# Reordering the 2,285 tasks of a delta-rule and gated feed-forward kernel, and which of its two DMA queues issues what

## The chip, the core and the metric

The kernel runs on one core of one Trainium2 chip. A core has TensorE (PE in the profile; PEld is its loading of weights), VectorE (DVE), ScalarE (ACT), GpSimd (POOL) and SyncE (SP), each with its own instruction stream that is worked off in order, and 16 DMA engines that all queues share. The metric is device time of one launch in microseconds (us). The kernel before took 643.51 us (median of three runs: 641.13, 643.51, 645.41).

## The reference, cut to what matters

```python
# q, k, v: (4, 8, 768, 48); beta: (4, 8, 768)
k_n = k / (norm(k) + 1e-06)
for t in range(768):                     # a state of 48 x 48 per batch and head
    y[t] = q[t] @ state
    v_old = state.T @ k_n[t]
    state = state + beta[t] * outer(k_n[t], v[t] - v_old)
x = y as (3072 tokens, 384)
h = x @ w_in                             # 384 x 2048
out = (h * cos(h)) @ w_out               # 2048 x 384
```

(The layer works on all 2048 columns; the weights arrive as 64-bit numbers, of which the kernel makes 32-bit ones.)

## The kernel before, in words

**The work.** The recurrence is done in 24 chunks of 32 time steps, for all 32 pairs of batch and head at once. For chunk n, in short:

- `k`, `q`, `v` n: DMAs that load the chunk (`load`, L393; 4 DMAs each, 8 for `k` from chunk 6 on).
- `turn` n (L677) turns k and q on TensorE for the first six chunks, and `turn_out` copies them out of PSUM on ScalarE. From chunk 6 on there is no turn on TensorE: `blocks` n 0 and 1 (L421, 4 DMAs each) load k and q in pieces of 32 wide, and `turn_out` n is `turn_blocks` (L697): four transposes of VectorE that write the tile `kq_t`.
- `gram` n (L704) multiplies keys with keys and queries; `gram_keys` and `gram_queries` (L839) take it out of PSUM on VectorE.
- The inverse of a triangular matrix: chunks 0 and 1 by repeated doubling on TensorE (`double`, L788, six levels of two halves, with copies, transposes and sums between). For chunk pairs m from 1 on: `gram_put` writes the matrices to DRAM, `gram_get` m reads them in another layout, POOL inverts (`inv`, L898), `put` m writes the result to DRAM, `get` n (L924) reads it back into the tile `zt`, of which there is one.
- `state` n (L946), `right` n, `solve` n (L1015) on TensorE; `solve_out` on VectorE (L1053); `part_out` on ScalarE (L1062, its copies L1066); `update` n (L1068) on TensorE and `update_out` on VectorE, which writes the state that `state` n+1 reads. Chunks 2 and 3 have `solve_half` and `between` ahead of `solve`.
- `within` n (L1087), `within_out` on ScalarE, `features` n (L1121) turn the chunk's answer into columns of x, `features_out` copies them.

Two chunks make a pair p of 256 tokens for the feed-forward part. Pair 0 goes through `hidden` (L1143: a quarter of a hidden block of 512 columns each) and `output` (L1343, an output column's 16 matmuls one by one, f = 0 to 15, for two halves of the tokens). The other pairs use sums of inputs and of weights (`x_sum` L1229, `in_sums` L1276, `left_sum` L1412, `right_sum`), so that fewer products are needed: 20 `layer` tasks per pair (L1318, four matmuls each) with `layer_copy` on ScalarE (L1334) and `layer_add` on VectorE, and seven `product` tasks of two parts each (L1399, four matmuls per part), which `collect` (L1436; ScalarE L1442, VectorE L1455) adds up in one of two output tiles `o`. `store` p i (L1464) writes a tile to DRAM, which frees it. The gate h cos(h) between is `turns` (L1185), `rest` (L1192), `cos` (L1201) and `gate` (L1204).

The weights come in 28 pieces (`weights` t, `narrow_load`, L547): t = 0 to 11 belong to the first matrix, t = 12 to 27 to the second one, and piece 12 + f is read by output column f. Each piece is a DMA and three steps that make 32-bit numbers of it: `split` on ScalarE, `shift` on VectorE, `add` on POOL.

**What sets the order.** Every step is registered as a task with `add`: a key such as `("get", 11)`, the engine, what it depends on, and which buffers it makes and uses. 2,285 tasks are registered. `Order.run` (L227) then emits them one after the other in the order that is written out in `LINE`, a list of the tasks' numbers:

```python
line = [keys[int(i)] for i in self.LINE.split()]
for key in line:
    emit, deps, makes, uses = self.tasks[key]
    assert deps <= done, key
    ...
    emit()
```

So `LINE` fixes the order on every engine, and which buffer a task gets (the one freed longest ago). The set `OTHER` holds the keys of the tasks that go to the second of two places: for a transfer, ScalarE's queue in place of SyncE's (`queue`, L387); for a sum, POOL in place of VectorE or the reverse (`either`, L390); for `within_half`, ScalarE in place of VectorE.

```python
def queue(*key):
    return nc.scalar if key in Order.OTHER else nc.sync
```

At the end every instruction is pinned behind the one before it on its engine (`pin`, L1971), and the DMAs of SyncE and ScalarE are pinned in the one order in which `LINE` has them, also across the two queues. In the trace these DMAs signal their end on eight semaphores in turn, so a DMA that is issued waits until the eighth one before it has landed. There are 666 of them, 101 issued by ScalarE.

**Warm-ups.** `keep_warm` (L501) is a matmul of no use on a tile of ones, which does nothing once the first output column has begun. Five stand ahead of all tasks (`WARM_FIRST`); 15 more are tasks `warm` 0 to 14 (`WARMS`). Nine of these 15 stand ahead of the first output column in `LINE`.

Of the kernel before, what the change touches and what calls it, by code (L numbers as in the profile page):

```python
# [60 lines left out]
class Order:  # L61

    OTHER = {
        ('double_eye', 0), ('double_far', 0), ('double_eye', 1), ('gram_put', 3), ('inv', 1, 0),
        ('inv', 1, 2), ('put', 1), ('within_half', 3), ('gram_put', 4), ('k', 5),
        ('gram_get', 2), ('put', 2), ('v', 9), ('put', 4), ('gram_put', 10), ('blocks', 11, 1),
        ('put', 5), ('get', 14), ('v', 15), ('gram_put', 15), ('blocks', 16, 1), ('get', 18),
        ('k', 19), ('v', 19), ('get', 20), ('put', 10), ('get', 21), ('get', 22), ('v', 23),
        ('blocks', 23, 0), ('put', 11), ('store', 0, 0), ('in_sums', 0), ('in_sums', 1),
        ('x_sum', 1, 'd'), ('x_sum', 1, 'n'), ('x_sum', 1, 'm'), ('x_sum', 1, 'e'),  # L70
        ('x_sum', 1, 'k'), ('x_sum', 1, 'g'), ('x_sum', 1, 'i'), ('x_sum', 1, 'l'),
        ('x_sum', 1, 'f'), ('x_sum', 1, 'h'), ('x_sum', 1, 'b0'), ('left', 1, 2, 0),
        ('left', 1, 3, 0), ('left', 1, 3, 1), ('x_sum', 2, 'd'), ('x_sum', 2, 'n'),
        ('x_sum', 2, 'm'), ('x_sum', 2, 'e'), ('x_sum', 2, 'k'), ('x_sum', 2, 'g'),
        ('x_sum', 2, 'l'), ('left', 2, 4, 0), ('left', 2, 4, 1), ('x_sum', 3, 'd'),
        ('x_sum', 3, 'n'), ('x_sum', 3, 'm'), ('x_sum', 3, 'e'), ('x_sum', 3, 'k'),
        ('x_sum', 3, 'g'), ('x_sum', 3, 'i'), ('x_sum', 3, 'l'), ('x_sum', 3, 'h'),
        ('left', 3, 1, 1), ('left', 3, 3, 0), ('x_sum', 4, 'd'), ('x_sum', 4, 'n'),
        ('x_sum', 4, 'm'), ('x_sum', 4, 'k'), ('x_sum', 4, 'g'), ('x_sum', 4, 'i'),
        ('x_sum', 4, 'f'), ('x_sum', 4, 'h'), ('x_sum', 4, 'b0'), ('left', 4, 3, 0),  # L80
        ('left', 4, 3, 1), ('store', 4, 0), ('x_sum', 5, 'd'), ('x_sum', 5, 'n'),
        ('x_sum', 5, 'm'), ('x_sum', 5, 'g'), ('x_sum', 5, 'i'), ('x_sum', 5, 'l'),
        ('left', 5, 1, 0), ('left', 5, 3, 0), ('left', 5, 3, 1), ('store', 5, 0),
        ('x_sum', 6, 'd'), ('x_sum', 6, 'n'), ('x_sum', 6, 'e'), ('x_sum', 6, 'k'),
        ('x_sum', 6, 'g'), ('x_sum', 6, 'i'), ('left', 6, 4, 1), ('left', 6, 3, 1),
        ('store', 6, 1), ('x_sum', 7, 'd'), ('x_sum', 7, 'm'), ('x_sum', 7, 'k'),
        ('x_sum', 7, 'g'), ('x_sum', 7, 'l'), ('x_sum', 7, 'b0'), ('left', 7, 2, 0),
        ('left', 7, 3, 0), ('x_sum', 8, 'e'), ('x_sum', 8, 'k'), ('x_sum', 8, 'g'),
        ('x_sum', 8, 'i'), ('left', 8, 2, 0), ('left', 8, 2, 1), ('left', 8, 4, 1),
        ('left', 8, 3, 1), ('store', 8, 0), ('x_sum', 9, 'n'), ('x_sum', 9, 'k'),  # L90
        ('x_sum', 9, 'g'), ('x_sum', 9, 'i'), ('x_sum', 9, 'l'), ('x_sum', 9, 'f'),
        ('x_sum', 9, 'h'), ('x_sum', 9, 'b0'), ('left', 9, 1, 1), ('left', 9, 2, 1),
        ('left', 9, 3, 0), ('left', 9, 3, 1), ('store', 9, 0), ('x_sum', 10, 'n'),
        ('x_sum', 10, 'm'), ('x_sum', 10, 'k'), ('x_sum', 10, 'g'), ('x_sum', 10, 'i'),
        ('x_sum', 10, 'f'), ('left', 10, 4, 0), ('left', 10, 4, 1), ('left', 10, 3, 0),
        ('x_sum', 11, 'd'), ('x_sum', 11, 'm'), ('x_sum', 11, 'k'), ('x_sum', 11, 'i'),
        ('left', 11, 1, 0), ('left', 11, 1, 1), ('left', 11, 2, 1), ('left', 11, 4, 0),
        ('left', 11, 4, 1), ('left', 11, 3, 0), ('store', 11, 1), ('store_right', 11),
        ('weights', 2), ('weights', 4), ('weights', 5), ('weights', 9), ('weights', 11),
        ('weights', 12), ('weights', 13), ('weights', 14), ('weights', 17), ('weights', 18),  # L100
        ('weights', 20)
    }
# [1932 lines left out]
```

## Time and profile before

| | |
|---|---|
| median of three runs | 643.51 us (641.13, 643.51, 645.41) |
| the profiled execution | 639.35 us |
| its span, first to last instruction | 637.5 us |
| instructions | 24,379 |
| DMA traffic | 50.51 MB, mean 79 GB/s |

The profile is of one execution, which was faster than the median. Its lines carry an engine, the line of the code (of a helper, where one emits), the tile written and the tiles read (out<-in), the count (x4) and microseconds. PE is TensorE, PEld its weight load; SPq and ACTq are the DMA issues of SyncE and ScalarE. In a timeline the first number is the start in us from the beginning of the span and the second the duration; a bracket gives how long the engine stood idle before and what released it. In the list of waits the numbers are the total of the wait in us, how often, and the longest one. A row of a stretch A:B gives its length, then the busy time of PE, PEld, DVE, ACT and POOL with the count of instructions, the granted clock of TensorE as a share of full speed, the mean busy share of the 16 DMA engines, and GB/s.

### The profile page before, as it was taken

How to read it: one execution, taken by the hardware profiler on the slowest of the kernel's cores; microseconds unless marked ns; L12 is line 12 of the kernel's file. 1: busy time of each engine (PE TensorE's matmuls, PEld its weight loads, DVE VectorE, ACT ScalarE, POOL GpSimd, SP SyncE). 2: the span in 40 equal slices, each digit the busy share in tenths (PEclk: the TensorE clock that was granted, in tenths of full speed). 3: DMA queues.
4: the chain of work that ended last, by engine and by line, in shares of the span. 5: the costliest groups of instructions: out<-in, count | busy, mean ns of one | idle time of the engine just before them, and what ended most of it. 6: DMA issues, size and time to landing. Idle time of an engine off the chain costs nothing.

```text
span 637.5 us, 24379 instructions
## 1 busy us (share of the span) xinstructions
PE 604.4 (95%) x10276; PEld 561.9 (88%) x10276; DVE 484.1 (76%) x981; ACT 326.1 (51%) x608; POOL 436.1 (68%) x774
## 2 busy tenths in 40 slices
PE   7788897999999998899999999999999999999997
PEld 6567776886999998889999999999999999999997
DVE  6878865989999886677978788867778576645772
ACT  3746664554753653553853645655453454545440
POOL 5468888688888886884987887878866862121222
PEclk9999998999999999999999999999999999999999
DMA  8878665665645444327436254323232101100001
GB/s 178 209 182 208 142 130 128 142 86 75 105 83 89 70 68 97 68 35 127 64 53 112 46 90 83 62 35 68 47 56 54 34 6 21 35 3 25 1 26 26
DMA packets 215893, 50.51 MB, mean 79 GB/s; under 512 B 207512, under 2 KB 210856, under 8 KB 215784
## 3 DMA queue, kind: packets, MB, share of 16 engines
q1 hardware_dynamic: 175600, 37.10, 31.8%
q10 hardware_dynamic: 39976, 11.61, 8.7%
q8 instruction: 81, 1.33, 0.9%
q0 software_dynamic: 208, 0.25, 0.2%
q14 instruction: 28, 0.23, 0.1%
HBM read 38.68 MB, written 10.22 MB: 77 GB/s over the span
## 4 chain that ended last, share of the span: by engine, by line
PE 69%; DMA 13%; DVE 6%; SPq 5%; issue 2%; ACT 2%; POOL 1%; ACTq 1%; DVEq 0%; POOLq 0%
PE p_h L1322 26%; PE p_out L1403 24%; PE p_kq L959 3%; DMA qp<-in_k_dram 3%; PE p_s L1075 2%; DMA out_dram<-o 2%; DMA kp<-in_k_dram 2%; PE p_out L1345 2%; DMA qp<-in_q_dram 2%; SPq L427 2%; PE p_kq L1092 2%; PE p_g L715 2%; PE p_h L1403 2%; PE p_u L1033 2%; SPq L408 1%
## 5 line engine op out<-in xcount | busy, mean ns | idle before, releaser
L908 POOL TENSOR_TENSOR part<-z,gb 128x126 f32<-128x126 f32 (+24 forms) x317 | 141.0, 445 | 36.9 <-DMA gb<-g_dr 6.6
L915 POOL TENSOR_TENSOR z<-z,part 128x126 f32<-128x126 f32 (+24 forms) x317 | 145.4, 459 | 24.8
L1403 PE MATMUL p_out<-w_out,g_ffn 128*128 128x192 f32 x672 | 120.3, 328 | 0.1
L1403 PEld LDWEIGHTS p_out<-w_out,g_ffn 128*128 128x128 f32 x672 | 107.9, 190 | 1.0 <-ACT o L1442 0.2
L1322 PE MATMUL p_h<-x_sum,w_in 128*128 128x128 f32 x704 | 93.9, 279 | 0.9 <-DVE g_ffn L1339 0.5
L1185 ACT ACTIVATE turns<-g_ffn,quarter_turn 128x512 int32<-128x512 f32 x77 | 55.4, 721 | 76.5 <-DVE g_ffn L1339 27.4
L1201 ACT ACTIVATE turns<-turns,halfpi 128x512 f32<-128x512 f32 x96 | 68.4, 719 | 50.6 <-DVE turns L1192 43.4
L1322 PEld LDWEIGHTS p_h<-x_sum,w_in 128*128 128x128 f32 x704 | 86.2, 191 | 4.6 <-DVE g_ffn L1339 0.8
L1403 PE MATMUL p_out<-w_sum,g_ffn 128*128 128x192 f32 x496 | 88.2, 328 | 1.8 <-DVE o L1455 1.7
L1403 PEld LDWEIGHTS p_out<-w_sum,g_ffn 128*128 128x128 f32 x496 | 79.7, 190 | 2.7 <-DVE o L1455 1.9
L1339 DVE TENSOR_TENSOR g_ffn<-g_ffn,p_h 128x512 f32<-128x512 f32 x88 | 59.6, 681 | 24.5 <-PE p_h L1322 19.6
L1192 DVE SCALAR_TENSOR_TENSOR turns<-g_ffn,turns 128x512 f32<-128x512 f32 x77 | 57.2, 748 | 13.7 <-ACT turns L1185 13.1
L1204 DVE TENSOR_TENSOR g_ffn<-turns,g_ffn 128x512 f32<-128x512 f32 x77 | 58.7, 769 | 8.2 <-ACT turns L1201 8.2
L1322 PE MATMUL p_h<-x_sum,in_sum 128*128 128x128 f32 x440 | 59.1, 278 | 1.5 <-ACT p_h L1334 1.5
L1322 PEld LDWEIGHTS p_h<-x_sum,in_sum 128*128 128x128 f32 x440 | 54.6, 192 | 3.9 <-ACT p_h L1334 2.0
L1419 POOL TENSOR_TENSOR g_ffn<-g_ffn,g_ffn 128x512 f32<-128x512 f32 x20 | 26.8, 1346 | 41.1 <-PE p_out L1403 41.0
L1105 ACT COPY y<-p_kq 32x384 f32<-32x384 f32 x88 | 41.3, 470 | 19.8 <-PE p_kq L1092 17.6
L1455 DVE SCALAR_TENSOR_TENSOR o<-p_out,o 128x192 f32<-128x192 f32 x74 | 25.1, 351 | 32.1 <-PE p_out L1403 25.6
L606 POOL TENSOR_TENSOR knrm<-ksum,halves 128x16 f32<-128x16 f32 (+1 forms) x14 | 37.0, 2643 | 17.1 <-DVE ksum L594 16.4
L1322 PE MATMUL p_h<-x_ffn,w_in 128*128 128x128 f32 x352 | 46.8, 277 | 0.2 <-ACT p_h L1334 0.2
L1322 PEld LDWEIGHTS p_h<-x_ffn,w_in 128*128 128x128 f32 x352 | 43.4, 192 | 1.5 <-ACT p_h L1334 0.5
L1334 ACT COPY p_h<-p_h 128x512 f32<-128x512 f32 x44 | 25.3, 574 | 32.9 <-PE p_h L1322 22.4
(175 smaller groups left out, 1039.7 us busy)
## 6 DMA issues: line engine op xcount, KB each, us to landing
gb<-g_dr SPq DMA_DIRECT2D x18, 256.0 KB
vp<-in_v_dram SPq DMA_DIRECT2D x80, 48.0 KB
w_sum<-in_moe_w_out_dram SPq DMA_DIRECT2D x9, 384.0 KB
kp<-in_k_dram SPq DMA_DIRECT2D x136, 24.0 KB
out_dram<-o SPq DMA_DIRECT2D x16, 192.0 KB
qp<-in_k_dram SPq DMA_DIRECT2D x34, 64.0 KB
g_ffn<-in_moe_w_in_dram SPq DMA_DIRECT2D x4, 512.0 KB
qp<-in_q_dram SPq DMA_DIRECT2D x32, 64.0 KB
```

The lines of the kernel that those rows point to most:

```text
L606: nc.gpsimd.tensor_tensor(out=scales[m][2][:, part], in0=sums[m, part.start][:, 0:n], in1=halves[:, 0:n], op=ALU.pow,)
L908: eng.tensor_tensor(out=part, in0=z[:, 0:rows, j, None].to_broadcast(shape), in1=a[:, j, None, j + 1 :].to_broadcast(shape), op=ALU.mult,)
L915: eng.tensor_tensor(out=behind, in0=behind, in1=part, op=ALU.subtract)
L1105: nc.scalar.copy(by_parity(y[quarter(b)]), p_kq[quarter(b ^ 1), :, b % 2])
L1185: nc.scalar.activation(turns[p, f], hidden_of(p, f), AF.Identity, bias=quarter_turn, scale=TURN)
L1192: nc.vector.scalar_tensor_tensor(out=r, in0=hidden_of(p, f), scalar=TURN, in1=t, op0=ALU.mult, op1=ALU.subtract,)
L1201: nc.scalar.activation(r, r, AF.Sin, bias=halfpi, scale=2.0 * math.pi)
L1204: nc.vector.tensor_tensor(out=place(p, f), in0=step_of(rests.pop((p, f)), f), in1=step_of(hidden_of(p, f), f), op=ALU.mult,)
L1322: nc.tensor.matmul(p_h[:, e], in_block(*w)[:, e], x_of(p, b), start=new and e == 0, stop=True, skip_group_check=True,)
L1339: nc.vector.tensor_tensor(out=part_of(p, to), in0=part_of(p, one), in1=part_of(p, two), op=op)
L1403: nc.tensor.matmul(p_o, left(p, part, a)[:, e % 4], right(e, b), start=(e == 0), stop=(e == FT // 2 - 1), skip_group_check=True,)
L1419: either(("left", p, x, s), nc.vector, nc.gpsimd).tensor_tensor(out=left(p, s, to), in0=left(p, s, one), in1=left(p, s, two), op=op)
```

## The change: two lists and a count

The diff touches only the class `Order`. No function changes; the same tasks are emitted with the same operands.

```diff
     OTHER = {
-        ('double_eye', 0), ('double_far', 0), ('double_eye', 1), ('gram_put', 3), ('inv', 1, 0),
-        ('inv', 1, 2), ('put', 1), ('within_half', 3), ('gram_put', 4), ('k', 5),
...
-        ('weights', 2), ('weights', 4), ('weights', 5), ('weights', 9), ('weights', 11),
-        ('weights', 12), ('weights', 13), ('weights', 14), ('weights', 17), ('weights', 18),
-        ('weights', 20)
+        ('double_eye', 0), ('v', 2), ('gram_put', 2), ('within_half', 2), ('inv', 1, 0),
+        ('put', 1), ('within_half', 3), ('q', 4), ('gram_put', 4), ('gram_get', 2),
...
+        ('weights', 7), ('weights', 12), ('weights', 13), ('weights', 14), ('weights', 15),
+        ('weights', 19)
     }
 
-    WARM_FIRST, WARMS = 5, 15
+    WARM_FIRST, WARMS = 5, 20
     LINE = """
-0 26 27 9 10 11 2173 1 2 5 3 28 12 13 4 30 142 84 85 86 31 2177 143 32 2181 2185 29 89 33 35 87 174
...
```

Decoded, it comes to this.

- **Warm-ups:** 20 tasks in place of 15; 19 of them stand ahead of the first output column, where it was 9. With the five ahead of all tasks that is 24 effective ones in place of 14.
- **Queues:** ScalarE issues 128 of the 666 DMAs in place of 101: output stores 11 in place of 7, `v` 8 in place of 4, `weights` 7 in place of 11, and others. Counted in groups (one task's DMAs), ScalarE has 50 in place of 44, and from `store 0,0` on 33 in place of 25, without the last stores.
- **Sums:** of 121 `x_sum` 52 are on POOL in place of 45; of 88 `left` sums 30 in place of 33; one `right` sum, where there was none; one of `in_sums` in place of two; one of `double_eye` and `double_far` in place of three. Of the pieces of the half-size inverse (`inv 1`) one is on VectorE in place of two, of `within_half` two on ScalarE in place of one.
- **Order.** The order of all tasks. Three stretches of the DMAs follow (a star marks ScalarE's queue, the number in brackets counts the DMAs up to the task's last one):

```
up to 28, before: weights 0 (1), k 2 (5), weights 1 (6), q 2 (10), *weights 2 (11), weights 3 (12),
  k 3 (16), *weights 4 (17), q 3 (21), eye_load (22), v 0 (26), *weights 5 (27), weights 6 (28)
up to 29, after:  weights 0 (1), k 2 (5), weights 1 (6), weights 2 (7), k 3 (11), weights 3 (12),
  q 2 (16), weights 4 (17), v 0 (21), *weights 5 (22), q 3 (26), weights 6 (27), eye_load (28),
  *weights 7 (29)

101 to 152, before: *weights 18 (101), get 3 (109), weights 19 (110), *weights 20 (111),
  blocks 6,1 (115), weights 21 (116), blocks 6,0 (120), k 8 (128), weights 22 (129), blocks 7,1 (133),
  v 4 (137), blocks 7,0 (141), k 9 (149), weights 23 to 25 (152)
101 to 152, after:  *weights 18 (101), get 3 (109), blocks 6,0 (113), *weights 19 (114),
  weights 20 (115), weights 21 (116), k 8 (124), blocks 6,1 (128), blocks 7,0 (132), blocks 7,1 (136),
  *k 9 (144), v 4 (148), weights 22 (149), weights 23 to 25 (152)

320 to 418, before: get 9 (320), blocks 13,0 (324), blocks 14,0 (328), v 12 (332), gram_put 12 (335),
  k 15 (343), blocks 14,1 (347), blocks 15,0 (351), gram_put 13 (354), *put 5 (355), store 1,0 (356),
  gram_get 6 (358), get 10 (362), v 13 (366), k 16 (374), blocks 15,1 (378), get 11 (382), k 17 (390),
  store 2,0 (391), v 14 (395), k 18 (403), *k 19 (411), store 2,1 (412), gram_put 14 (415),
  *gram_put 15 (418)
320 to 417, after:  *get 9 (320), v 11 (324), blocks 14,0 (328), v 12 (332), *gram_put 12 (335),
  k 15 (343), store 1,0 (344), *v 13 (348), gram_put 13 (351), put 5 (352), gram_get 6 (354),
  blocks 14,1 (358), get 10 (362), blocks 15,0 (366), get 11 (370), k 16 (378), store 2,0 (379),
  *v 14 (383), k 17 (391), store 2,1 (392), blocks 15,1 (396), k 18 (404), gram_put 14 (407),
  *blocks 16,0 (411), gram_put 15 (414), put 6 (415), gram_get 7 (417)
```

TensorE's tasks at the start (d 0.1.0 is `double` of chunk 0, level 1, half 0; h 0.2 is part 2 of block 0 of `hidden`):

```
before: warm 0-4, turn 0, gram 0, turn 1, d 0.0.1, gram 1, d 0.0.0, d 0.1.1, warm 5, d 1.0.0, d 0.2.1,
  d 1.0.1, d 0.3.1, turn 2, d 0.1.0, d 1.1.0, gram 2, warm 6, d 0.4.1, d 0.2.0, turn 3, d 1.1.1,
  d 0.5.1, gram 3, d 0.3.0, d 1.2.0, d 1.2.1, d 0.4.0, d 0.5.0, state 0, warm 7-8, d 1.3.0, solve 0,
  update 0, d 1.3.1, within 0, d 1.4.0, turn 4, d 1.4.1, features 0, d 1.5.1, d 1.5.0, state 1,
  gram 4, h 0.0-3, solve 1
after:  warm 0-1, turn 0, warm 2, gram 0, warm 3, turn 1, gram 1, warm 4-5, d 0.0.0, d 0.0.1, warm 6-8,
  d 0.1.0, d 0.1.1, d 1.0.1, warm 9, turn 2, d 0.2.0, d 0.2.1, d 1.1.1, gram 2, d 1.0.0, turn 3,
  d 0.3.0, d 1.1.0, d 1.2.1, d 0.3.1, gram 3, d 1.2.0, d 1.3.1, d 0.4.0, warm 10, d 0.4.1, warm 11,
  state 0, d 0.5.1, d 0.5.0, d 1.4.1, warm 12, solve 0, warm 13, d 1.3.0, update 0, within 0, turn 4,
  warm 14-15, features 0, state 1, d 1.5.1, h 0.0, gram 4, d 1.4.0, h 0.1, d 1.5.0, h 0.2, solve 1
```

And what TensorE has between steps that wait for one another:

| from, to | before | after |
|---|---|---|
| solve_half 2 to between 2 | nothing | h 6.3 |
| between 2 to solve 2 | output 0,0 column 1, h 8.0, h 8.1 | h 8.0 to h 8.2 |
| solve 2 to within 2 | nothing | output 0,0 column 0, h 8.3 |
| within 2 to update 2 | nothing | h 10.0 |
| solve 4 to update 4 | output 0,0 column 12, one layer, output column 13, within 4 | one layer, within 4 |
| solve 8 to update 8 | both parts of a product of pair 2, within 8 | one layer, within 8 |
| within 8 to features 8 | update 8, six layers, both parts of a product, state 9, gram 12, solve 9 | update 8 and one layer |

Output column 10 of the first half, which reads `weights 22`, stands behind `update 3` in the new order.

More of the change, by code (lines that the diff above doesn't have):

```diff
@@ L70 @@
[L70 to L98, printed above, removed]
-        ('weights', 2), ('weights', 4), ('weights', 5), ('weights', 9), ('weights', 11),
@@ new lines @@
+        ('blocks', 20, 1), ('gram_put', 20), ('v', 21), ('gram_get', 10), ('put', 10),
+        ('v', 22), ('v', 23), ('put', 11), ('get', 23), ('store', 0, 0), ('right', 2, 2),
+        ('in_sums', 4), ('x_sum', 1, 'd'), ('x_sum', 1, 'n'), ('x_sum', 1, 'm'),
+        ('x_sum', 1, 'e'), ('x_sum', 1, 'k'), ('x_sum', 1, 'g'), ('x_sum', 1, 'i'),
+        ('x_sum', 1, 'f'), ('x_sum', 1, 'b0'), ('left', 1, 1, 0), ('x_sum', 2, 'd'),
+        ('x_sum', 2, 'n'), ('x_sum', 2, 'm'), ('x_sum', 2, 'e'), ('x_sum', 2, 'k'),
@@ new lines @@
+        ('x_sum', 2, 'g'), ('x_sum', 2, 'i'), ('x_sum', 2, 'l'), ('x_sum', 2, 'b0'),
+        ('left', 2, 4, 0), ('x_sum', 3, 'd'), ('x_sum', 3, 'l'), ('x_sum', 3, 'f'),
+        ('x_sum', 3, 'h'), ('x_sum', 3, 'b0'), ('left', 3, 4, 1), ('store', 3, 0),
+        ('store', 3, 1), ('x_sum', 4, 'i'), ('x_sum', 4, 'f'), ('x_sum', 4, 'h'),
+        ('left', 4, 4, 0), ('left', 4, 4, 1), ('left', 4, 3, 0), ('left', 4, 3, 1),
+        ('x_sum', 5, 'd'), ('x_sum', 5, 'm'), ('x_sum', 5, 'e'), ('x_sum', 5, 'k'),
@@ new lines @@
+        ('x_sum', 5, 'g'), ('x_sum', 5, 'f'), ('x_sum', 5, 'b0'), ('left', 5, 1, 0),
+        ('left', 5, 2, 0), ('left', 5, 1, 1), ('left', 5, 2, 1), ('left', 5, 4, 0),
+        ('left', 5, 3, 0), ('store', 5, 0), ('x_sum', 6, 'd'), ('x_sum', 6, 'n'),
+        ('x_sum', 6, 'm'), ('x_sum', 6, 'k'), ('x_sum', 6, 'i'), ('x_sum', 6, 'f'),
+        ('x_sum', 6, 'h'), ('x_sum', 6, 'b0'), ('left', 6, 1, 1), ('left', 6, 2, 1),
+        ('store', 6, 0), ('store', 6, 1), ('x_sum', 7, 'n'), ('x_sum', 7, 'e'),
@@ new lines @@
+        ('x_sum', 7, 'i'), ('x_sum', 7, 'h'), ('x_sum', 7, 'b0'), ('left', 7, 2, 1),
+        ('left', 7, 4, 0), ('left', 7, 4, 1), ('left', 7, 3, 1), ('store', 7, 0),
+        ('store', 7, 1), ('x_sum', 8, 'n'), ('x_sum', 8, 'e'), ('x_sum', 8, 'k'),
+        ('x_sum', 8, 'g'), ('x_sum', 8, 'f'), ('x_sum', 8, 'h'), ('x_sum', 8, 'b0'),
+        ('left', 8, 2, 0), ('left', 8, 3, 1), ('store', 8, 1), ('x_sum', 9, 'd'),
+        ('x_sum', 9, 'm'), ('x_sum', 9, 'i'), ('x_sum', 9, 'f'), ('x_sum', 9, 'h'),
@@ new lines @@
+        ('x_sum', 9, 'b0'), ('left', 9, 1, 0), ('left', 9, 2, 1), ('left', 9, 4, 1),
+        ('store', 9, 0), ('x_sum', 10, 'd'), ('x_sum', 10, 'k'), ('x_sum', 10, 'l'),
+        ('x_sum', 10, 'f'), ('x_sum', 10, 'h'), ('left', 10, 1, 0), ('left', 10, 2, 0),
+        ('left', 10, 3, 0), ('left', 10, 3, 1), ('x_sum', 11, 'k'), ('x_sum', 11, 'i'),
+        ('x_sum', 11, 'f'), ('x_sum', 11, 'h'), ('x_sum', 11, 'b0'), ('left', 11, 1, 0),
+        ('left', 11, 4, 1), ('store', 11, 1), ('store_right', 11), ('weights', 5),
```

7 lines of the change are left out of this document (3 added, 4 removed), and 208 rows, old and new, of the table LINE.

## Prediction, made before the change was run

> **What bounds the kernel.** I read the page first, then the busy time by stretches, then who waited for whom, then the timelines of the stretches in which TensorE stands.
>
> ```profile
> span 637.5 us, 24379 instructions
> PE 604.4 (95%) x10276; PEld 561.9 (88%) x10276; DVE 484.1 (76%) x981; ACT 326.1 (51%) x608; POOL 436.1 (68%) x774
> ```
>
> TensorE is the bound: 604.4 of 637.5 us, 33.1 us idle. The same matmuls run after the change, so it can win only idle time and time at a low clock. The stretches (span, then the busy time of PE, PEld, DVE, ACT and POOL, granted clock, DMA share, GB/s) say where that lies:
>
> ```profile
> 0.00:20.00 20.00, 14.19 (x230) 11.44 (x230) 13.15 (x40) 7.90 (x16) 10.27 (x18) 1.00 0.87 187
> 20.00:40.00 20.00, 15.74 (x372) 13.57 (x373) 16.73 (x48) 13.78 (x30) 11.21 (x9) 1.00 0.82 196
> 40.00:60.00 20.00, 15.44 (x501) 13.27 (x500) 16.54 (x49) 10.40 (x22) 13.99 (x21) 1.00 0.80 216
> 76.00:83.00 7.00, 5.48 (x248) 4.62 (x239) 4.14 (x7) 3.36 (x7) 6.06 (x16) 1.00 0.83 199
> 100.00:120.00 20.00, 15.65 (x235) 12.71 (x235) 14.88 (x35) 9.13 (x18) 15.12 (x28) 0.91 0.64 141
> 104.00:108.00 4.00, 2.69 (x53) 2.50 (x58) 3.05 (x9) 1.06 (x2) 3.29 (x10) 0.66 0.64 150
> 240.00:280.00 40.00, 35.03 (x579) 32.75 (x579) 26.93 (x56) 20.82 (x40) 30.89 (x55) 1.00 0.36 68
> 280.00:320.00 40.00, 39.66 (x769) 37.46 (x769) 33.04 (x70) 21.09 (x40) 28.84 (x58) 1.00 0.57 88
> ```
>
> Idle is span less PE: 5.81, 4.26 and 4.56 in the head (14.63), 1.52 in 76 to 83, 4.35 in 100 to 120, 4.97 in 240 to 280, 0.34 after. Behind the 4.35 the clock falls (0.66 in 104 to 108): 20 us at 0.91 on the mean lose 20 x 0.09 = 1.8 us. Everything outside the head follows from transfers that come late, or from short round trips.
>
> **Part 1, the blocks of chunk 7.** Up to `get 3` both orders issue the same 109 transfers. SyncE and VectorE then:
>
> ```profile
> 91.14 1.65 SPq L550 DMA_DIRECT2D w_sum<-in_moe_w_out_dram  x1
> 92.83 2.03 SPq L427 DMA_DIRECT2D qp<-in_q_dram  x4
> 94.91 3.04 SPq L408 DMA_DIRECT2D vp<-in_v_dram  x4
> 97.99 2.04 SPq L427 DMA_DIRECT2D qp<-in_k_dram  x4
> ```
> ```profile
> 103.10 1.42 DVE L702 STREAM_TRANSPOSE kq_t<-qp 128x256 f32<-128x256 f32 x4 [5.75 <-DMA qp<-in_k_dram]
> ```
>
> SyncE issues without a pause. The second half of blocks 7 is issued by 100.03, has landed at 103.10, and VectorE, whose queue is in order, waits 5.75 us at its transposes; TensorE needs the PSUM bank that the next VectorE step frees, and stands 4.35. The new order puts `weights 22` and `v 4` behind the blocks: 1.65 + 3.04 = 4.69 us of SyncE's time fewer ahead of them. That is more than 4.35, so the idle goes, and the 1.8 with it: **-6.15** (ends: -6.15 and 0). VectorE still waits some 1.1 us (5.75 - 4.69). Late next is `weights 22`, moved past `v 4` and `k 9` (which goes to ScalarE's queue): its piece is read by output column 10, which the new order puts behind update 3, so nobody waits.
>
> **Part 2, stores and blocks near 240 to 272.** The waits of TensorE, the wait of ScalarE, and SyncE's queue:
>
> ```profile
> PE p_out L1403 <- DVE o L1455: 1.7, 1, 1.7
> PE p_h L1322 <- ACT p_h L1334: 1.7, 2, 1.5
> PE p_u L1033 <- DMA zt<-z_dr: 1.7, 2, 0.9
> ```
> ```profile
> ACT o L1442 <- DMA out_dram<-o: 5.4, 2, 3.8
> ...
> ACT turns L1185 <- DMA kp<-in_k_dram: 4.7, 1, 4.7
> ```
> ```profile
> 239.54 0.58 SPq L1470 DMA_DIRECT2D out_dram<-o  x1
> ...
> 251.64 3.79 SPq L408 DMA_DIRECT2D kp<-in_k_dram  x8
> 255.47 3.11 SPq L427 DMA_DIRECT2D qp<-in_q_dram  x4
> 258.68 3.03 SPq L939 DMA_DIRECT2D zt<-z_dr  x4
> 261.75 3.77 SPq L408 DMA_DIRECT2D kp<-in_k_dram  x8
> 265.62 0.66 SPq L1470 DMA_DIRECT2D out_dram<-o  x1
> ```
>
> Store 1,0 (issued 239.54) frees an output tile that a collect needs; TensorE waits 1.7. In the new order 12 transfers fewer stand ahead of it; at 3.79/8 = 0.47 us each, 5.7 us. `get 11` (258.68) brings the inverse for solve 11; `k 16` and half of blocks 15 no longer stand ahead: 3.79 + 3.11 = 6.9 us earlier, against a wait of 1.7 (at most so much, since its buffer is free only when solve 10 has run). Store 2,0 (265.62) held ScalarE 3.8 us at a collect, and with it a copy for TensorE (1.5 of the 1.7); `k 17`, 3.77 us, now stands behind it. All three waits are covered: **-4.9** (1.7 + 1.7 + 1.5; ends -4.9 and -3.2, one of them left). What is moved behind (`k 16`, `k 17`, blocks 15) is read by later chunks; if it were late, the 5.75 above is what it looks like on VectorE.
>
> **Part 3, round trips.** In 76 to 83 TensorE waits 1.52 us for short answers, each time with nothing of its own between question and answer. The new order puts one hidden part ahead of `between 2`, an output column and a hidden part ahead of `within 2`, and another ahead of `update 2`: **-1.5** (ends -1.5 and 0). The other way: from solve 4 and solve 8 to their updates, and from within 8 to features 8, the new order leaves fewer matmuls. The chain solve, solve_out, part_out, update takes
>
> ```profile
> L1066 ACT ACTIVATE u<-u_all,consts 128x384 f32<-128x384 f32 x42 | 23.4, 605 | 9.1 <-DVE u_all L1053 9.0
> ...
> L1053 DVE TENSOR_TENSOR u_all<-p_u,bs 128x384 f32<-128x384 f32 x22 | 12.1, 549 | 6.7 <-PE p_u L1033 4.8 <-PE p_u L1028 1.8
> ```
> ```profile
> 248.91 1.06 PE L1322 MATMUL p_h<-x_sum,in_sum 128*128 128x128 f32 x8
> 249.80 1.06 PE L1322 MATMUL p_h<-x_ffn,in_sum 128*128 128x128 f32 x8
> ```
>
> 0.55 + 2 x 0.6 = 1.75, with handovers an estimated 2.05; beside it lie one layer (0.89 from start to start) and one `within` of about 0.75 (estimate, from its size beside the layer's): 0.4 short, twice, and about 0.5 at features 8: **+1.3** (ends 0 and +3).
>
> **Part 4, the head.** Ten more warm-up matmuls run before the first output column (24 instead of 14, counting the five that stand in the preamble). `q 2` ends as transfer 16 instead of 10, `q 3` as 26 instead of 21, and `turn 3` stands ahead of the third level of the doubling instead of behind part of it.
>
> ```profile
> 17.66 0.70 PE L503 MATMUL p_out<-o 128*128 128x256 f32 x2
> 31.01 0.66 PE L682 MATMUL p_t<-consts,kp 128*128 128x128 f32 x4
> 39.67 1.13 PE L503 MATMUL p_out<-o 128*128 128x256 f32 x4
> ```
> ```profile
> 19.24 6.04 DMA qp<-in_q_dram
> ```
> ```profile
> 18.88 2.87 SPq L408 DMA_DIRECT2D qp<-in_q_dram  x4
> ...
> 22.34 3.59 SPq L408 DMA_DIRECT2D vp<-in_v_dram  x4
> ```
>
> A warm-up costs 1.13 - 0.70 = 0.43 us, ten of them 4.3, nothing where TensorE stands anyway (14.63 us here), all of it where it doesn't. `q 3` was issued by 21.75 and landed at 25.28 (19.24 + 6.04), 3.53 later. Transfer 26 of the old order was issued by 25.93, so `q 3` now lands near 29.5; 480 KB more lie ahead of it than at that place before, 2.5 us at 196 GB/s: 32.0 at most. `turn 3` ran at 31.01: 1.5 earlier to 1.0 later. Behind it more doubling is still to do, but three tasks of the doubling are put behind state 1. I take half of the warm-ups as paid (about half of them stand directly ahead of a task that waited before) and the turn as unmoved: **+2** (ends: -3, all warm-ups covered and the turn and the deferred tasks won; +5.5, all paid and the turn 1.0 late).
>
> **Part 5, queues.** Issues on ScalarE go from 101 to 128 of 666: 27 x 0.47 = 12.7 us of its time, beside 311 us in which it idles. Sums moved between VectorE and POOL (7 more x sums on POOL, 3 fewer left sums, one right sum) nearly cancel: nothing, as long as the inverses on POOL come in time; there is one per two chunks, and the work ahead of each is within 2% in both orders.
>
> **Sum:** -6.15 - 4.9 - 1.5 + 1.3 + 2 = -9.25. The profiled execution took 639.35 us (span 637.5 and 1.85 around it), so 630.1; the median of the three runs, 643.51, lies 4.16 above that execution: **634.3**. TensorE stays busy behind each gain, so each carries to the end.
>
> **Two rules weighed.** The Trainium skill, "DMA: Bandwidth & Descriptors", section "Issuing engines are not separate DMA queues", says that all issuers share the same 16 DMA engines and that another issuer saves only sequencer time. The trace has engines 0.80 to 0.87 busy in the head, where I count no gain from transfers, and 0.64 in 100 to 120, where SyncE's issue is solid. If the engines, not the issue, set the arrival at 100, it would stay: that is the second rival. The same skill, "TensorE: Matmul & The Clock Gate", section "What's actually happening", says that about 3.4 us without work halve the clock; the trace agrees at 100 (4.35 idle, then 0.66). By it a long stand in the head would cost clock too: the third rival.
>
> **The rivals.**
> 1. ScalarE blocked (the other side): a transfer in its queue holds all behind it, and from `store 0,0` on the new order has 33 such groups, the old one 25 (without the last stores). For: the store that held it 3.8 us cost TensorE 1.5. Against: eight loads held it 4.7 us near 282, and 280 to 320 shows 0.34 idle in all. At 1.5 each, six such groups eat the gain; with 12 the time is 634.3 + 18 = 652.3.
> 2. The arrival at 100 stays, set by the transfers themselves: 634.3 + 6.15 = 640.4. Against: 384 KB fewer lie ahead, and DMA is at 0.64.
> 3. The head: all warm-ups paid, `turn 3` stands over 4 us and the clock falls as at 100: 634.3 + 3.5 + 1.8 = 639.6. For: `q 3` up to 32.0, with a turn that nothing can pass.
> 4. New stalls as large as the old, since a searched order meets other delays than it reckoned with: 643.5. For: the old order has stalls too. Against: they lie where 0.47 us per transfer and its landing do not fit, and there the new one leaves room.
>
> That the change doesn't do what it says is excluded by the count of 101 and 128.
>
> **How the numbers follow.** Forecast 0.62 (its own range 628 to 640, from the ends of the head and one wait of part 2 left), rival 1 0.13, rival 2 0.07, rival 3 0.07, rival 4 0.11. 1% (6.4 us, to 637.1) is about what a measurement of this kernel can tell from no change. Faster by more: 0.56 of the forecast's 0.62 and 0.02 of the rivals: 0.58. Slower by over 1%: rival 1 less 0.01: 0.12. The rest, 0.30, is the same. The range for 8 in 10 is 627 to 647: it leaves out rival 1 and 0.05 below.
>
> **What would show it.** VectorE's wait at the transposes of chunk 7 under 2 us and the clock at 1.00 through 120 (part 1); no wait over 0.5 us of a collect for an output store, nor of solve 11 (part 2); idle of the first 60 us between 10 and 16 (part 4). Wrong: ScalarE standing at its transfers with TensorE idle behind it, or a first layer that starts over 3 us later than before.

## The result and the profile after

The new kernel takes 634.64 us (median of four runs, 633.69 to 635.52) beside 642.32 us of the old one in the same group: ratio 0.9893, 95% interval 0.9849 to 0.9938, so 4 to 10 us less. A later group of runs gave 0.9906 (0.9878 to 0.9934). The forecast time of 634.3 is met; the forecast gain (9.2 us, a ratio of 0.986) is larger than both measured ones. One run of the whole study, of the kernel with the old choice of queues (686.5 us), fell in a slower state and is left out of that kernel's ratio. The profiled execution took 635.52 us, 3.8 less than the old kernel's. The head of the new kernel's page:

```profile
span 633.7 us, 24406 instructions
...
PE 611.1 (96%) x10296; PEld 565.9 (89%) x10296; DVE 481.1 (76%) x969; ACT 326.8 (52%) x610; POOL 430.6 (68%) x784
```

TensorE is idle 22.6 us in place of 33.1, but busy 6.7 us longer. Ten more warm-ups at 0.43 us are an estimated 4.3 of these; the mean clock is 0.997 in both profiles, so the rest stays open. Its busy time by stretches:

```profile
0.00:20.00 20.00, 16.13 (x241) 12.94 (x243) 13.62 (x41) 8.13 (x15) 8.65 (x14) 1.00 0.89 188
20.00:40.00 20.00, 16.93 (x396) 14.09 (x393) 16.59 (x49) 13.17 (x28) 10.48 (x11) 1.00 0.87 205
40.00:60.00 20.00, 14.51 (x401) 11.61 (x400) 13.14 (x37) 9.48 (x20) 13.33 (x22) 0.94 0.74 190
76.00:83.00 7.00, 6.90 (x170) 6.33 (x169) 5.94 (x11) 4.21 (x9) 5.97 (x13) 1.00 0.60 110
100.00:120.00 20.00, 19.35 (x379) 15.13 (x378) 18.76 (x39) 13.51 (x26) 18.08 (x31) 1.00 0.80 172
104.00:108.00 4.00, 3.35 (x37) 1.66 (x44) 3.02 (x7) 3.91 (x8) 3.37 (x9) 1.00 0.82 212
240.00:280.00 40.00, 39.45 (x742) 37.33 (x740) 32.14 (x63) 23.56 (x45) 33.56 (x67) 1.00 0.47 78
280.00:320.00 40.00, 40.00 (x686) 38.48 (x685) 34.05 (x67) 22.83 (x43) 30.30 (x59) 1.00 0.50 83
```

The stretches of which parts 1 to 3 spoke look as they said: idle 0.65 at 100 to 120 (it was 4.35) with the clock at 1.00, 0.55 at 240 to 280 (4.97), 0.10 at 76 to 83 (1.52; the same steps of chunk 2 now stand at 78.7 to 88.8 us, and TensorE waits at none of them). From 40 to 60 the clock fell to 0.94, which the sum had not foreseen. VectorE's transposes of chunk 6 and 7 now run as one row, with no bracket: neither waits for the blocks. In 240 to 280 one wait of TensorE is left; those for the output tile and the copy are gone.

```profile
100.81 2.72 DVE L702 STREAM_TRANSPOSE kq_t<-qp 128x256 f32<-128x256 f32 x8
```
```profile
PE p_u L1033 <- DMA zt<-z_dr: 0.5, 1, 0.5
```

So far this reads as a full success of parts 1 to 3. But these three parts are 12.55 us in the prediction's terms, against 3.3 that it charges for shorter round trips and the head, and the medians fell by 6.4 to 7.7. What they were worth is not in these rows.

### The profile page after: what moved, and what is told of

It reads as the page before. It is cut to its first block, busy times and chain, and to the rows that moved or that the text cites. A ratio compares the mean times of both kernels' runs of the same rounds, so it can differ in the third digit from the quotient of the medians.

```text
span 633.7 us, 24406 instructions
## 1 busy us (share of the span) xinstructions
PE 611.1 (96%) x10296; PEld 565.9 (89%) x10296; DVE 481.1 (76%) x969; ACT 326.8 (52%) x610; POOL 430.6 (68%) x784
## 4 chain that ended last, share of the span: by engine, by line
PE 69%; DMA 13%; POOL 8%; DVE 3%; issue 2%; ACT 2%; SPq 2%; ACTq 1%; POOLq 0%; DVEq 0%
PE p_out L1403 27%; PE p_h L1322 25%; DMA kp<-in_k_dram 3%; POOL part L908 3%; PE p_kq L959 3%; POOL z L915 3%; PE p_s L1075 2%; DMA qp<-in_q_dram 2%; PE p_kq L1092 2%; PE p_g L715 2%; PE p_out L1345 2%; DMA w_sum<-in_moe_w_out_dram 2%; PE p_h L1403 2%; DMA w_out<-in_moe_w_in_dram 2%; PE p_u L1033 1%
## 5 line engine op out<-in xcount | busy, mean ns | idle before, releaser
L908 POOL TENSOR_TENSOR part<-z,gb 128x126 f32<-128x126 f32 (+23 forms) x321 | 139.9, 436 | 50.1 <-DMA gb<-g_dr 20.7
L915 POOL TENSOR_TENSOR z<-z,part 128x126 f32<-128x126 f32 (+23 forms) x321 | 146.9, 458 | 25.2
L1403 PE MATMUL p_out<-w_out,g_ffn 128*128 128x192 f32 x672 | 121.7, 329 | 0.3 <-DVE g_ffn L1419 0.3
L1403 PE MATMUL p_out<-w_sum,g_ffn 128*128 128x192 f32 x496 | 88.8, 328 | 0.2
L1185 ACT ACTIVATE turns<-g_ffn,quarter_turn 128x512 int32<-128x512 f32 x77 | 54.7, 719 | 45.8 <-DVE g_ffn L1204 19.1
L1204 DVE TENSOR_TENSOR g_ffn<-turns,g_ffn 128x512 f32<-128x512 f32 x77 | 55.5, 726 | 18.3 <-ACT turns L1201 18.1
L1419 POOL TENSOR_TENSOR g_ffn<-g_ffn,g_ffn 128x512 f32<-128x512 f32 x14 | 17.9, 1278 | 43.7 <-PE p_out L1403 27.2
```

What stands on the lines that cost most here:

```text
L908: eng.tensor_tensor(out=part, in0=z[:, 0:rows, j, None].to_broadcast(shape), in1=a[:, j, None, j + 1 :].to_broadcast(shape), op=ALU.mult,)
L915: eng.tensor_tensor(out=behind, in0=behind, in1=part, op=ALU.subtract)
L1185: nc.scalar.activation(turns[p, f], hidden_of(p, f), AF.Identity, bias=quarter_turn, scale=TURN)
L1204: nc.vector.tensor_tensor(out=place(p, f), in0=step_of(rests.pop((p, f)), f), in1=step_of(hidden_of(p, f), f), op=ALU.mult,)
L1403: nc.tensor.matmul(p_o, left(p, part, a)[:, e % 4], right(e, b), start=(e == 0), stop=(e == FT // 2 - 1), skip_group_check=True,)
```

## Experiments

All ran in three groups, each beside runs of the old kernel on the same chip (639.47, 641.41 and 642.04 us). The last columns are the mean clock over all runs of the kernel, and that of the old one in its group.

| kernel | median us (runs) | ratio to the old one | clock | old |
|---|---|---|---|---|
| before_again | 639.90 (12) | 1.0000 (0.9977 to 1.0024) | 0.990 | 0.991 |
| after_v2_sync | 633.84 (12) | 0.9916 (0.9885 to 0.9947) | 0.996 | 0.991 |
| after_few_warm | 634.91 (12) | 0.9928 (0.9900 to 0.9955) | 0.990 | 0.991 |
| head_before | 635.77 (12) | 0.9944 (0.9912 to 0.9977) | 0.992 | 0.991 |
| after_again | 634.98 (6) | 0.9906 (0.9878 to 0.9934) | 0.997 | 0.988 |
| after_blocks14 | 633.62 (6) | 0.9883 (0.9854 to 0.9911) | 0.996 | 0.988 |
| v2_blocks14 | 634.85 (6) | 0.9886 (0.9859 to 0.9914) | 0.997 | 0.988 |
| before_part2 | 637.98 (8) | 0.9940 (0.9914 to 0.9966) | 0.988 | 0.988 |
| before_part1 | 640.95 (12) | 0.9988 (0.9959 to 1.0018) | 0.990 | 0.988 |
| after_old_queues | 676.51 (6) | 1.0537 (1.0506 to 1.0567) | 0.971 | 0.988 |
| after_half_warm | 635.67 (6) | 0.9911 (0.9876 to 0.9945) | 0.993 | 0.988 |
| head_before2 | 637.29 (7) | 0.9928 (0.9902 to 0.9954) | 0.989 | 0.988 |

Across groups only the ratios are compared. Line numbers shift by up to four between kernels (L1181 here is L1185 there), as the lists above them differ in length. Diffs of `LINE` are shown decoded.

### v 2 back on SyncE's queue

The new head first looked slow: by an estimate (nominal durations of the matmuls added up, without warm-ups) TensorE had done 40 us of its useful work some 6 us later than in the old one. ScalarE's timeline of the new kernel offers a cause: it stands 4.95 us behind `v 2`, which is in its own queue.

```profile
45.91 3.08 ACTq L408 DMA_DIRECT2D vp<-in_v_dram  x4
49.03 0.47 ACT L1105 COPY y<-p_kq 32x384 f32<-32x384 f32 x1 [4.95 <-DMA vp<-in_v_dram]
```

```diff
     OTHER = {
-        ('double_eye', 0), ('v', 2), ('gram_put', 2), ('within_half', 2), ('inv', 1, 0),
+        ('double_eye', 0), ('gram_put', 2), ('within_half', 2), ('inv', 1, 0),
```

> The new kernel with one key taken out of OTHER: the loads of v 2 go to SyncE's queue, at the same place in the order of the DMAs. Theory A (what the new head loses against the old one is ScalarE, which stands 4.9 us at within_out 0 behind v 2 in its own queue, and the half clock that TensorE's stand then brings): that wait is under 1 us, the clock is 1.00 from 56 to 62, features 0 and hidden 0.0 come some 2 to 3 us earlier, and the time is 3 to 5 us below the new kernel's 634.6, so 630 to 632. Theory B (the head loses by the ten warm-up matmuls, 0.43 us each, and ScalarE's stand lies beside them): within 1 us of the new kernel, 633.6 to 635.6.

The wait for `v 2` went (2.84 us for TensorE are left in its place), but the time did not follow: 0.9916, no lower than the new kernel's two ratios, and 633.84 us is theory B's figure. By the same estimate the profile has TensorE 2 to 3 us ahead at 40 us of work, and no longer ahead at 260 us. Theory A falls as an account of the time. Its stretches around solve 10 show where the lead went:

```profile
244.00:248.00 4.00, 4.00 (x87) 3.83 (x86) 3.63 (x7) 1.24 (x2) 2.89 (x5) 1.00 1.16 203
248.00:252.00 4.00, 2.52 (x46) 2.21 (x45) 2.88 (x10) 0.57 (x1) 3.15 (x11) 0.99 0.38 53
252.00:256.00 4.00, 4.00 (x16) 3.91 (x14) 1.16 (x2) 1.85 (x3) 3.53 (x9) 0.59 0.50 76
```

TensorE arrives at solve 10 early, stands 1.48 us there (it waits for `get 10`), and then works at a clock of 0.59.

### Ten warm-ups fewer

```diff
-        add(("warm", i), "PE", 0.43, keep_warm, [("warm", i - 1)] if i else [])
+        add(("warm", i), "PE", 0.43, keep_warm if i < 9 else lambda: None, [("warm", i - 1)] if i else [])
```

> The new kernel with only the first nine warm-up tasks doing a matmul, as many as before the change; warm 9 to 18 emit nothing, the order of all else is the new one. Theory A (most of the ten stand where TensorE waits anyway, so they cost little; the head's loss is ScalarE behind v 2): the time falls by 0 to 1.5 us, 633 to 635, or rises by up to 2 if TensorE's clock falls more often without them. Theory B (they are paid in full): it falls by 3 to 4.3 us, 630 to 632.

No gain: 0.9928. The clock column gives a reason: 0.990 over twelve runs, as in the old kernel, where the new kernel with all warm-ups has 0.996 to 0.997. Its stretch from 40 to 60 us:

```profile
40.00:60.00 20.00, 14.16 (x376) 12.14 (x377) 12.66 (x36) 8.85 (x18) 12.40 (x21) 0.74 0.74 180
```

At 0.74 in place of 0.94, up to 20 x 0.20 = 4.0 us more are lost here than in the new kernel. Theory B is wrong. Theory A's time is met, and so is its clause that the clock falls more often without the ten. What one warm-up costs is not shown: in the profiles TensorE stands 27.5 us in all without them and 22.6 with them, so less idle time and a higher clock together give back about what the matmuls take.

### The old head before the new rest, twice

```diff
 # LINE, decoded
-new order
+old order and queues up to features 1, then all other tasks in the new order
```

> The old order and queues up to features 1 (68.8 us in the old trace), and from there the rest of the tasks in the new order with the new queues. Theory A and the progress of TensorE in both traces (at this place the new kernel is 5.8 us behind the old one, and all that it wins, it wins behind this place): 5 to 6 us below the new kernel, 628 to 630. The rival (the new rest wins only because the transfers behind the head were already issued by its own head, with q 3, weights and blocks 6 in another order): the splice loses some of it again at blocks 6 and 7, and the time is 633 or more.

0.9944, no faster than the new kernel. The splice had a flaw: six warm-ups of the rest came to stand right behind features 1, where TensorE has work. The second one has the old nine only:

> The old order and queues up to features 1 and the new ones from there, this time with the nine warm-ups of the old order and no others. It differs from the new kernel with nine warm-ups (634.9, mean clock 0.990) only in the order of the head. If the new head's order of turns, doubling and transfers is itself slower, as the profiles suggest (TensorE has done 40 us of its work after 66 to 67 us in the old order and after 68 to 74 in the new ones): 2 to 4 us faster than that kernel, 631 to 633. If the new order's head is as good and those profiles differ by clock and warm-ups only: 634 to 636.

0.9928, the same as the new kernel with nine warm-ups (0.9928). (As a time, 637.29 lies above both ranges; the old kernel is 2.6 us slower in this group.) At an equal number of warm-ups the two heads are worth the same; the new order of turns and doubling is neither better nor worse by more than some 2.5 us.

### The old and the new kernel again

> The old kernel unchanged, for a second profile of it: its runs so far lie between 638.9 and 645.4 us, the new kernel's four between 633.7 and 635.5. Theory C (the old order has a stall that comes out differently in each execution, at the blocks of chunk 7 near 100 us or at the stores near 240 to 272, where TensorE waits for a transfer): this profile differs from the first one by as much as its time does, and the difference lies in these two stretches. Theory D (the spread is in the head, where the transfers fill the DMA engines): the difference lies in the first 60 us. Its time should be 639 to 645 either way.

The time is the same, the profile is not. In the first profile VectorE waited 5.75 us at chunk 7; here:

```profile
101.74 1.43 DVE L702 STREAM_TRANSPOSE kq_t<-qp 128x256 f32<-128x256 f32 x4 [1.00 <-DMA qp<-in_k_dram]
```

Instead the inverse of chunks 2 and 3 (`get 2`) came late, and ScalarE's copy behind solve_half 2 started at 77.97 in place of 76.25. The rows of the old kernel's first and second profile:

```profile
76.25 0.48 ACT L1001 COPY g_ffn<-p_w 128x384 f32<-128x384 f32 x1 [0.39 <-PE p_w L989]
```
```profile
77.97 0.48 ACT L1001 COPY g_ffn<-p_w 128x384 f32<-128x384 f32 x1 [2.22 <-PE p_w L989]
```

Theory C is right on chunk 7 and wrong on the stores, theory D sees only a part: the executions differ in which late transfer of the first 110 us stops TensorE. Busy time by large stretches (columns as in the prediction), the old kernel's second profile, then the new kernel's first and second:

```profile
0.00:60.00 60.00, 46.88 (x1093) 39.72 (x1093) 45.94 (x132) 32.26 (x66) 35.26 (x46) 0.97 0.82 195
60.00:120.00 60.00, 53.88 (x1307) 45.49 (x1306) 48.81 (x94) 35.70 (x70) 50.57 (x82) 0.97 0.66 143
120.00:240.00 120.00, 118.27 (x2185) 106.13 (x2183) 106.58 (x211) 65.11 (x126) 101.27 (x197) 1.00 0.51 83
240.00:280.00 40.00, 35.39 (x583) 33.14 (x583) 27.83 (x56) 20.81 (x40) 31.21 (x56) 1.00 0.36 69
```
```profile
0.00:60.00 60.00, 47.57 (x1027) 38.64 (x1028) 43.35 (x125) 30.78 (x63) 32.46 (x46) 0.98 0.84 194
60.00:120.00 60.00, 57.18 (x1392) 48.39 (x1391) 46.56 (x91) 37.33 (x75) 52.12 (x89) 0.99 0.68 141
120.00:240.00 120.00, 117.54 (x2163) 104.50 (x2162) 107.11 (x205) 63.35 (x122) 102.85 (x197) 1.00 0.51 85
```
```profile
0.00:60.00 60.00, 47.56 (x1091) 38.87 (x1095) 43.73 (x125) 30.59 (x64) 32.31 (x45) 0.97 0.84 194
60.00:120.00 60.00, 55.79 (x1347) 47.17 (x1335) 48.46 (x92) 37.64 (x76) 53.59 (x89) 1.00 0.69 143
120.00:240.00 120.00, 118.94 (x2173) 105.97 (x2173) 105.51 (x204) 64.00 (x123) 104.46 (x201) 1.00 0.50 84
240.00:280.00 40.00, 39.22 (x792) 37.01 (x791) 32.34 (x63) 22.57 (x43) 33.92 (x65) 1.00 0.50 82
```

> The new kernel unchanged, as the measure for the other runs of this group and for a second profile. It should be 634 to 636 us beside an old kernel of 639 to 640. Theory A: ScalarE stands 4 to 5 us at within_out 0 behind v 2 in this profile too, and TensorE's clock falls behind it. If instead the head of this profile is as fast as the old one's, that stand was one execution's accident.

The stand is there again. ScalarE's copies follow the last of the four issues of `v 2` at once, as in the first profile:

```profile
46.13 3.01 ACTq L408 DMA_DIRECT2D vp<-in_v_dram  x4
49.18 0.47 ACT L1105 COPY y<-p_kq 32x384 f32<-32x384 f32 x1 [4.49 <-PE p_t L682]
```

The bracket names TensorE, but the copy starts when the issues end, at 49.14 (48.99 in the first profile). So the stand was no accident. What theory A hung on it does not hold: here the clock falls ahead of it (0.79 in 36 to 44) and is 1.00 behind it (44 to 62), and with `v 2` moved the time stayed. A gain read from one execution of the first 120 us is a sample; from 240 to 280 the two profiles of each kernel agree (idle 4.97 and 4.61; 0.55 and 0.78).

### Part 1 alone, in the old kernel

```diff
 # DMAs, decoded from LINE
-  weights 22, blocks 7,1, v 4, blocks 7,0, k 9
+  blocks 7,1, blocks 7,0, v 4, weights 22, k 9
```

(split 22 and shift 22 move with it.)

> The old kernel with only part 1 of the prediction done: weights 22 and v 4 stand behind blocks 7,0 in the order of the DMAs; split 22 and shift 22, which read weights 22, stand behind features_out 3 and gram_queries 7 so that they hold nobody. The prediction's theory (the stand at 100 and the half clock behind it belong to the old order in every execution): 6 us faster than the old kernel, and the mean granted clock over the runs rises from 0.990 to 0.995 or more. Theory G (in some executions the wait is short, as in the second profile of the old kernel with 1.0 us, and then the loss and the low clock lie at other places of the first 100 us): 2 to 4 us faster, and the clock rises by less than 0.004.

0.9988: from 1.2 us slower to 2.6 us faster. Its profile, of its slowest execution, shows the stand in the other place. ScalarE's timeline and TensorE's waits there:

```profile
82.50 0.48 ACT L1000 COPY g_ffn<-p_w 128x384 f32<-128x384 f32 x1 [4.27 <-PE p_w L988]
```
```profile
PE p_w L988 <- DMA w_sum<-z_dr: 3.2, 2, 2.3
```

ScalarE waits 4.27 us for solve_half 2, which waits for `get 2` (the read of `z_dr`). Three profiles of the old order show one wait or the other: ScalarE's at `get 2` short and VectorE's at blocks 7 long (0.39 and 5.75 in the first, 0.16 and 5.52 in part 2's), or the reverse (2.22 and 1.00 in the second). Here the blocks come early by the edit, and the wait at `get 2` is the longest of all. That fits theory G, whose 2 to 4 us lie at the edge of the interval or beyond it.

### Part 2 alone, in the old kernel

```diff
 # DMAs, decoded from LINE
-  k 15, blocks 14,1, blocks 15,0, gram_put 13, put 5, store 1,0, gram_get 6, get 10, v 13, k 16, blocks 15,1, get 11, k 17, store 2,0
+  k 15, store 1,0, blocks 14,1, blocks 15,0, gram_put 13, put 5, gram_get 6, get 10, v 13, get 11, k 16, blocks 15,1, store 2,0, k 17
```

> The old kernel with only part 2 of the prediction done: store 1,0 right behind k 15, get 11 ahead of k 16 and blocks 15,1, and store 2,0 ahead of k 17; all else as before. The prediction's theory: the three waits of TensorE (1.7 at the collect's tile, 1.7 at solve 11, 1.5 at the copy behind the store) go, 4 to 5 us, so 635 to 636 beside an old kernel of 639.5 to 640. The rival (inverse 5 and the collects hold the old order as well, so that TensorE waits a few us further on for the same thing): under 2 us, 638 or more.

0.9940, so 3.9 us (2.2 to 5.5). The prediction's mechanism holds. The three waits are gone; what is left of the 4.97 is 1.80, at solve 10, which waits for `get 10` and did not wait in the first profile:

```profile
240.00:280.00 40.00, 38.20 (x611) 36.30 (x610) 32.01 (x61) 21.94 (x42) 32.50 (x60) 1.00 0.39 68
```
```profile
PE p_u L1032 <- DMA zt<-z_dr: 1.8, 2, 1.1
```

### What comes next at solve 10

`put 5` is issued when POOL ends the inverse (242.0 us in the new kernel, 241.5 with `v 2` moved, though TensorE is 2 us ahead there: it is free for solve 10 at 249.3, where the new kernel starts it at 251.3), and `gram_get 6` and `blocks 14,1` stand between it and `get 10`.

```diff
 # DMAs, decoded from LINE
-  put 5, gram_get 6, blocks 14,1, get 10
+  blocks 14,1, put 5, gram_get 6, get 10
```

> The new kernel with one group of four transfers moved: blocks 14,1 stands ahead of put 5 in the order of the DMAs (SyncE is idle there), no longer between put 5 and get 10. Theory E (in the new order the inverse of chunk pair 5, which POOL ends at 242, sets the start of solve 10, by way of put 5 and get 10; a lead won before is lost there): get 10 is issued 2.4 us earlier and solve 10 no longer waits for it, but in this kernel it waited only some 0.5 to 0.8 us, so the time falls by 0 to 1.5 us. The rival (solve 10 is set by TensorE's and VectorE's own work, and get 10 comes in time either way): no wait changes, within 0.5 us.

> The new kernel with v 2 on SyncE's queue and blocks 14,1 ahead of put 5. With v 2 alone moved, the profile has TensorE 3.2 us ahead of the new kernel at 70 us, still 2 us ahead at 240, and 0.6 behind at 258, after two stands of 1.1 us at solve 10 and half the clock for some 3.6 us. Theory E: with get 10 issued 2.4 us earlier those stands and the clock's loss are gone and the lead is kept: 2.5 to 4 us below the kernel with v 2 alone moved, 630 to 632. The rival (the lead is lost by something else near 250, as the clock falling by itself, or by VectorE): the same loss near 250 and a time of 633 to 635.

The profile of the first shows TensorE at solve 10 with no wait for `get 10`, at 248.6 us, earlier than in any other, and the clock at 1.00:

```profile
248.00:252.00 4.00, 3.94 (x53) 3.64 (x52) 3.04 (x9) 2.15 (x4) 3.30 (x10) 1.00 0.54 73
```

That shows theory E's mechanism. Its worth is not settled: 0.9883 and 0.9886 beside 0.9906 in the same group, with intervals that overlap. The second kernel missed its 630 to 632 (634.85), and its profile doesn't test theory E, since its head came late (solve 10 at 253.7, and nothing to lose). These two are the fastest by ratio, no more can be said.

### Fewer warm-ups at chosen places

The kernel with `blocks 14,1` moved, and warm 9, 11, 13, 16, 17 and 18 without a matmul.

> The new kernel with blocks 14,1 ahead of put 5, and with six warm-ups (9, 11, 13, 16, 17, 18) that emit nothing; kept are those that stand directly ahead of a wait of TensorE in the trace (10, 12, 14, 15) and the first nine. Theory F (each warm-up costs its 0.43 us of TensorE's time, and pays only by keeping the clock up across a wait): the mean clock stays near 0.996 and the time falls by 2.6 us from 633.6, to 630.5 to 632. The rival (the clock depends on the sum of the warm-ups, not on their places): the mean clock falls to about 0.992 and the time stays at 633 to 635.

0.9911 and a clock of 0.993: no gain; the rival is the nearer one. Six warm-ups are worth 2.6 us of matmuls, and without them the clock lost 0.003, at most 1.8 us of 633.

### The old choice of queues in the new order

```diff
     OTHER = {
-        keys of transfers as in the new kernel (50 groups)
+        keys of transfers as in the old kernel (44 groups)
```

> The new order with the old choice of queues for all transfers: the 44 groups that ScalarE issued before the change go to ScalarE, all others to SyncE; sums and within_half as in the new kernel. It undoes the part of the change that gives ScalarE more transfers. The prediction's part 5 (that part is worth nothing): within 1 us of the new kernel, 634 to 636. The rival (ScalarE's share relieves SyncE's queue, 27 issues of 0.47 us, where the order is laid out for it): 2 us or more slower, 637 or above. The other rival (ScalarE blocked is a cost of the new choice): 1.5 us or more faster, 633 or below.

676.5 us, 5.4% slower than the old kernel and some 41 us slower than the new one: the largest effect of the study, from the choice of queues alone. The longest wait of ScalarE, and its timeline there:

```profile
ACT turns L1181 <- DMA zt<-z_dr: 11.1, 1, 11.1
```
```profile
553.00 0.72 ACT L1197 ACTIVATE turns<-turns,halfpi 128x512 f32<-128x512 f32 x1
559.49 0.38 ACTq L916 DMA_DIRECT2D z_dr<-z  x1
562.97 1.82 ACTq L935 DMA_DIRECT2D zt<-z_dr  x4
564.83 1.33 ACT L1181 ACTIVATE turns<-g_ffn,quarter_turn 128x512 int32<-128x512 f32 x2 [11.11 <-DMA zt<-z_dr]
```
```profile
567.55 2.93 PE L1399 MATMUL p_out<-w_out,g_ffn 128*128 128x192 f32 x8 [4.69 <-DVE g_ffn L1415]
```

`put 11` waits for POOL's inverse, `get 22` for `put 11` to land. Both are in ScalarE's queue, and ScalarE's own work is behind them: 11.1 us. VectorE's `rest` of that block, the sum behind it (L1415) and the product wait in turn, and TensorE stands 4.69. In the new kernel `get 22` is on SyncE's queue, which has nothing else to do there. The Trainium skill, "DMA: Bandwidth & Descriptors", section "Issuing engines are not separate DMA queues", says that another issuer saves only sequencer time; here the choice of issuer was worth 41 us, and at this place the cost is what stands behind a waiting transfer on the engine that issues it. How much of the 41 came about so is not shown: in the profiles TensorE's idle time rose from 22.6 to 51.0 us and its busy time from 611.1 to 622.8, at a mean clock of 0.974 in place of 0.997. The first rival's time (637 or above) is met too, and SyncE's longer queue may have a share.

## Why the prediction was right in time, and wrong in its sum

- **Part 1** failed at "so the idle goes, and the 1.8 with it". The wait went as worked out. Its worth, alone in the old kernel, was 0.8 us (a loss of 1.2 to a gain of 2.6), not 6.15. With it falls "TensorE stays busy behind each gain, so each carries to the end", for the first 110 us: there the next late transfer takes the place of the one removed, and the second profile of the old kernel has the same time with 1.00 us of that wait. The first layer starts at 109.99 and 109.07 us in the new kernel's two profiles, and at 108.50 and 105.86 in the old one's. Rival 2 had the right size (no gain) with another reason (it counts 384 KB less ahead; with `v 4` it is 576).
- **Part 2** was right: 3.9 (2.2 to 5.5) for 4.9. All three waits went; what it did not foresee is the new one at solve 10 (1.80).
- **Part 3**: the waits of 1.5 us are gone in the new profile; no run took this part out by itself, so their worth is not shown. Nor is the loss of 1.3: idle at 120 to 240 is 2.46 and 1.06 in the new kernel's two profiles, 1.07 and 1.73 in the old one's.
- **Part 4** failed at "I take half of the warm-ups as paid". On balance they cost nothing (0.9928 without the ten, 0.9893 and 0.9906 with them); what the sum lacked is their return. By the mean clock over the runs, the old kernel loses up to (1 - 0.9882) x 640 = 7.6 us, the new one in the same group up to (1 - 0.9967) x 633 = 2.1 (estimates: a share of the span). These are upper bounds: over 174 runs on record, each beside the mean of its kernel and group, the time falls by 2.9 us (2.3 to 3.6) per 0.01 of clock, where a share of the span would be 6.4. With nine warm-ups the new order has the old clock. `turn 3` ran 1.9 to 2.3 us earlier (29.11 and 28.70 for 31.01), and head_before2 shows no gain from the new head.
- **Part 5** failed at "nothing" as a statement on queues: in the new order the old choice costs 41 us. What the new choice is worth in the change as made, no run shows. Rival 1 named the mechanism, but priced a blocked ScalarE at 1.5; the runs show 4.69 for one place.
- **The 4.16** added from profiled execution to median were in part clock: that execution had 0.997, where the old kernel's mean is 0.988 to 0.991. By a share of the span that would be 4 to 6 us, but the four of 47 runs of the old kernel in one group that had 0.997 took 637.9 us on the mean, 1.6 less than all of them. The new order with its warm-ups does not share the low clock, so that part should not have been carried over.

That the time came out right is luck, twice over. Median beside median the gain was 7.7 us, 1.5 short of the forecast 9.2, and the base of 643.51 (three runs) lay 1.2 above the group's median of 642.32: the two errors cancel. In the second group the gain was 6.4. And within the sum, some 5 us too much in part 1 stand against what the warm-ups give back and what part 4 charged for them.

Where the 6.4 us between the medians of the second group come from, worked out from the runs: clock -5.5 by a share of the span or -2.5 by the slope above, ten warm-ups at most +4.3, part 2 -3.9, which leaves -1.3 or -4.3 for all else, part 3 among it. That split is an estimate and not settled. What runs show by themselves is that part 2 brings 3.9 us in the old kernel, that part 1 brings little there, and that the clock rises with the ten warm-ups.

Open: what a warm-up costs and returns by itself, what else is in the 6.4 us, why the old head stops now at one transfer and now at another, and whether `blocks 14,1` ahead of `put 5` is worth its 1 us.

## What to carry to other kernels

A wait seen in one execution of a stretch that is bound by transfers is not a price: take the part out by itself, or look at a second profile, before adding it to a sum. Check the granted clock over all runs beside the profile's; warm-up matmuls have to be charged and credited. And a transfer belongs on a compute engine's queue only if what it waits for is done by the time the engine reaches it; order and choice of queue are one decision.
